# Sliding-window attention on quarter tiles of TensorE, in a fused attention and snake-MLP kernel on one core

## The chip, the cores and the metric

The kernel runs on one core of one Trainium2 chip. TensorE multiplies matrices (its weight loads are counted apart, as PEld), ACT evaluates functions such as exp and sine, DVE does elementwise work and reductions, GpSimd (POOL) and SyncE issue transfers. The metric is the device time of one execution in microseconds. Times per stage come from one profiled execution.

## The reference: what is computed

There are 8 batches, 8 heads, 576 positions and 64 elements per head. Scores are kept within 32 positions of the diagonal and in the rows and columns of 8 global positions; all else is masked away. The attention output becomes 4608 tokens of 512 features, and an MLP with a snake activation follows.

```python
scores = scale * np.matmul(q, k.transpose(0, 1, 3, 2))
mask = np.abs(pos[:, None] - pos[None, :]) <= window
mask = mask | is_global[:, None] | is_global[None, :]
attn = softmax(np.where(mask, scores, -1e9))
x = (attn @ v).transpose(0, 2, 1, 3).reshape(B * S, H * D)
h = x @ w_in                      # 512 -> 2048
s = np.sin(alpha * h)
out = (h + s * s / (alpha + 1e-9)) @ w_out   # 2048 -> 512
```

## The kernel before, in words

**Tiles of attention.** Keys of a head are cut into 12 tiles of 48. A key tile meets a window of 120 query columns (`WCOL`): twice 60, for the even and the odd positions, with 4 columns for global queries in each 60. Each key tile also carries the 8 global keys, so 56 of 64 rows are in use. Two heads form a pair (`NHP` = 4 pairs). A pair is worked on as one 128 x 128 matmul with two zero blocks: `KX` holds the keys of head 0 in rows and columns 0 to 63 and of head 1 in rows and columns 64 to 127, zeros elsewhere, and `VX` likewise for the values. Per pair, `scores` (line 739) runs 12 such matmuls of 120 columns in three groups of 4, each into a PSUM bank of a ring of two. ACT takes exp of a group (line 747), with a sum over the row as a second result, which an instruction of its own reads out. DVE multiplies by the 0/1 mask (line 750). `products` (line 781) multiplies the result E with the values (key 0, into the tile `zn`) and with `OB`, two blocks of ones (key 1, into `zd`, the denominators); 2 of the 12 windows cross the middle and are cut in two, so there are 14 matmuls per key. `inverse` (lines 807 and 810) makes 1/denominator as exp(-ln), `normalise` (line 813) multiplies, and `sums` (line 791) adds up the partial rows of the global queries.

**The MLP.** `gemm1` (line 969) multiplies 4 x 128 weights blocks of `w_in` with the 576 tokens of a batch for each of 16 blocks of hidden features, in halves of 288 columns; the blocks take the PSUM tiles `zn`, `zr`, `zd` in turn. ACT takes the sine, ACT or DVE squares it, DVE adds h (line 1016). `gemm2` (line 1029) is a generator: each step is one matmul of 512 columns, and every 16 steps ACT copies a result (line 1035) that SyncE stores.

**The order.** Nothing reorders the program; each engine runs its instructions in the order in which they are written. `phase_a(b+1, b)` emits the attention of batch b+1, and pours in steps of `gemm2(b)` with `fill(n)`: `START` steps before the first scores, `PER_SCORES` after each group, `MIDST` near the end, 53 in all for most batches; `gemm1` takes 16 more (`PER_GROUP`). For the attention of batch 1 there are other numbers (`LATE`, `GROUP_LATE`). What isn't used up is carried on, and the last of it follows the last batch. `products` of a pair come one pair later than its scores. `warm` issues matmuls without use where the attention has nothing beside it.

**Loads.** GpSimd issues, in one queue: V straight into `VX` (`load_v`, line 390, 4 transfers a pair, 16 a batch), the casts of K and Q to bf16 in DRAM (`cast_qk`, line 328), the weights (lines 407 and 413), and copies of global keys and queries (`place_globals`, lines 368 and 373). SyncE issues the transposes of the casts (`turn_qk`, line 337), the global rows of V (`load_vg`, line 399, 8 a batch), gathers, and the stores. Each queue has 8 semaphores for its transfers, and a transfer waits for the one that used its semaphore before, eight earlier. In the attention of batch 0, a copy of one element (`seen`) holds GpSimd until the transpose for batch 1 has landed; after it come the second half of `w_in` and V of batch 1. Batch 0's K and Q go through TensorE transposes (line 587).

**Guards.** The kernel keeps bounds for the whole run and takes a general path if one is broken: row sums of exp (`EA`) and of the inverses (`RA`), and the norm of each token against the largest column norm of `w_in` times alpha (`square_x`, `token_norms`, `square_w`, `column_norms`, `judge`), since the sine takes limited arguments. The general path didn't run in any execution shown.

Of the kernel before, what the change touches and what calls it, by code (L numbers as in the profile page):

```python
# [16 lines left out]
P = 128  # L17
# [12 lines left out]
LIM_SUM = float(2.0**50)  # L30
LIM_REC = float(2.0**40)
TINY = float(2.0**-60)
# [215 lines left out]
def kernel(  # L248
# [16 lines left out]
    NT12 = S // KT  # L265
    NHP = H // 2
# [19 lines left out]
    pairp = mctx.enter_context(tc.tile_pool(name="pairp", bufs=2))  # L286
# [4 lines left out]
    srp = mctx.enter_context(tc.tile_pool(name="srp", bufs=4))  # L291

    VX = [main.tile([P, NHP, NT12, P], DT.bfloat16, name=f"VX{i}") for i in range(2)]
    KX = [main.tile([P, NHP, NT12, P], DT.bfloat16, name=f"KX{i}") for i in range(2)]
# [6 lines left out]
    OB = main.tile([P, P], DT.bfloat16, name="OB")  # L301
    MASK = main.tile([P, NT12, WCOL], DT.bfloat16, name="MASK")
# [7 lines left out]
    tiny = main.tile([P, 1], DT.float32, name="tiny")  # L310
    SQ = main.tile([P, CT * S], DT.bfloat16, name="SQ")
    W2 = main.tile([P, DFF], DT.bfloat16, name="W2")
    limit = main.tile([P, 1], DT.float32, name="limit")
    EA = main.tile([P, B * NHP * 3], DT.float32, name="EA")
    RA = main.tile([P, B * NHP], DT.float32, name="RA")
    XC = main.tile([P, B], DT.float32, name="XC")
    XCG = main.tile([P, 1], DT.float32, name="XCG")
# [24 lines left out]
    def place(b, which, t, y, copy, hps=slice(0, NHP)):  # L342
# [10 lines left out]
        else:  # L353
            copy(
                out=KX[b % 2][rows, hps, :, t * D + y * 24 : t * D + y * 24 + 24],
# [8 lines left out]
    def place_globals(b):  # L364

        for t in range(2):
            rows = slice(t * D, (t + 1) * D)
            nc.gpsimd.tensor_copy(
                out=KX[b % 2][rows, :, :, t * D + KT : t * D + KT + NG],
                in_=kTg[rows, :, None, :, b].to_broadcast([D, NHP, NT12, NG]),  # L370
            )
        for y in range(2):
            nc.gpsimd.tensor_copy(
                out=globals_of(b, slice(0, P), y),
                in_=qTg[:, :, None, y::2, b].to_broadcast([P, NHP, 7, 4]),
            )
# [8 lines left out]
    def load_v(b, hps=range(NHP)):  # L385
        for hp in hps:
            for t in range(2):
                for y in range(2):
                    r = t * D + y * 24
                    nc.gpsimd.dma_start(  # L390
                        out=VX[b % 2][r : r + 24, hp, :, t * D : t * D + D],
                        in_=v[b, 2 * hp + t].rearrange("(i a y) d -> y a i d", a=24, y=2)[y],
                    )

    def load_vg(b):
        for h in range(H):
            t = h % 2
            src = VGb[b::B, h * D : (h + 1) * D] if b else VG0[h::H]
            nc.sync.dma_start(
                out=VX[b % 2][t * D + KT : t * D + KT + NG, h // 2, :, t * D : t * D + D],  # L400
                in_=src[:, None, :].to_broadcast([NG, NT12, D]),
            )
# [48 lines left out]
    qpos = setup.tile([P, NT12, 2, 24], DT.float32, name="qpos")  # L451
    nc.gpsimd.iota(qpos[:], pattern=[[KT, NT12], [1, 2], [2, 24]], base=0, channel_multiplier=0,
# [40 lines left out]
    def clear(t):  # L493
        n = t.shape[1]
        nc.scalar.activation(out=t, in_=zero[:].to_broadcast([P, n]), func=AF.Copy, scale=0.0)

    nc.scalar.preload_act_table_set("natural_log_exp_and_others")
    clear(QX[0][:].rearrange("p h y c -> p (h y c)").bitcast(DT.float32))
    vflat = VX[0][:].rearrange("p h i c -> p (h i c)").bitcast(DT.float32)
    kflat = KX[0][:].rearrange("p h i c -> p (h i c)").bitcast(DT.float32)  # L500
# [689 lines left out]
```

## Time and profile before

| | |
|---|---|
| median of 3 runs | 381.93 us (381.09 to 382.87) |
| profiled execution, span from first to last instruction | 379.3 us, 8582 instructions |
| median less that span | 2.6 us |
| mean granted TensorE clock | 0.994 |
| transfers | 38.08 MB in 103579 packets |

The time of the profiled execution is known as its span; what lies around it is taken from the median. In rows of groups, the columns are line, engine, operation, output and inputs, shapes and count, then busy time in us and mean ns of one, then idle time before them and what ended it. In the timeline they are start, length, engine, line, group, and idle time before it in brackets. A matmul's length has its way through the array in it, so that a group's length is more than its count times the pace.

### The profile page before, as it was taken

The page shows a single profiled execution, that of the slowest core. Times are in us where ns is not written, and L with a number is a line of the kernel's source. Part 1 is how long each engine was busy: PE and PEld are TensorE (multiplying, and loading weights), DVE is VectorE, ACT ScalarE, POOL GpSimd, SP SyncE. Part 2 cuts the span into 40 slices and gives each one's busy share as a digit, 9 for nine tenths or more (in the row PEclk, how much of TensorE's full clock was granted, in tenths as well). Part 3 has the DMA queues.
Part 4 walks back from the last instruction along what each step waited for, and adds up shares of the span by engine and source line. Part 5 has one row for each costly group of instructions (what it writes and reads, how often), then busy time and mean ns, then how long its engine had stood idle before and what let it go on. Part 6 is the DMA issues. An engine that isn't in the chain of part 4 may idle for free. (4 is left out here: it accounts for less than half of the span.)

```text
span 379.3 us, 8582 instructions
## 1 busy us (share of the span) xinstructions
PE 338.6 (89%) x3124; PEld 231.9 (61%) x3172; DVE 288.8 (76%) x615; ACT 294.0 (77%) x563; POOL 130.4 (34%) x203
## 2 busy tenths in 40 slices
PE   2578967998998899899989999999999998999893
PEld 2466645765566666676666766676676665775341
DVE  5787897589789887988888788888888876589400
ACT  6889797899889688788878887879788888675110
POOL 7981695677277002840086007720000000000001
PEclk9999999999999999999999999999999999999997
DMA  7998999999988772799069923828111010101221
GB/s 121 117 184 172 152 166 173 170 207 146 204 163 76 134 124 65 92 109 204 28 85 105 193 58 45 84 31 156 50 35 29 0 55 32 29 3 29 56 84 48
DMA packets 103579, 38.08 MB, mean 100 GB/s; under 512 B 94138, under 2 KB 98250, under 8 KB 103082
## 3 DMA queue, kind: packets, MB, share of 16 engines
q0 software_dynamic: 56640, 18.56, 42.2%
q1 hardware_dynamic: 46890, 18.89, 23.1%
q8 instruction: 27, 0.44, 0.5%
q14 instruction: 22, 0.18, 0.2%
HBM read 37.15 MB, written 17.83 MB: 145 GB/s over the span
## 5 line engine op out<-in xcount | busy, mean ns | idle before, releaser
L1029 PE MATMUL zo<-w_out,H 128*128 128x512 bf16 x528 | 142.5, 378 | 2.0
L969 PEld LDWEIGHTS <-w_in 128*128 128x128 bf16 x1024 | 99.2, 97 | 49.3 <-issue 17.6
L390 POOL DMA_DIRECT2D VX<-in_v_dram x128 | 84.0, 667 | 106.5 <-PE zd L781 89.6
L1029 PEld LDWEIGHTS <-H 128*128 128x128 bf16 x576 | 52.0, 97 | 37.3
L747 ACT ACTIVATE E<-ring 128x480 bf16<-128x480 f32 x96 | 54.2, 568 | 23.3 <-PE ring L739 22.8
L969 PE MATMUL zn<-xT,w_in 128*128 128x288 bf16 x384 | 57.3, 285 | 5.6 <-DVE H L1016 4.1
L969 PE MATMUL zr<-xT,w_in 128*128 128x288 bf16 x320 | 47.9, 285 | 1.3 <-DVE H L1016 0.6
L969 PE MATMUL zd<-xT,w_in 128*128 128x288 bf16 x320 | 46.6, 285 | 1.7 <-DVE H L1016 1.7
L750 DVE TENSOR_TENSOR E<-E,MASK 128x480 bf16<-128x480 bf16 x96 | 36.0, 408 | 14.8 <-ACT E L747 13.5
L1016 DVE SCALAR_TENSOR_TENSOR H<-s,recipT,zn 128x576 bf16<-128x576 bf16 x48 | 39.1, 814 | 10.5 <-ACT s L1010 6.2
L1005 ACT ACTIVATE sb<-zn,alphaT 128x576 bf16<-128x576 f32 (+1 forms) x48 | 35.6, 742 | 13.3 <-PE zn L969 9.8
L1057 POOL DMA_INDIRECT out_dram<-osb,grow x1 | 1.0, 1007 | 126.1 <-SPq L1158 126.1
L1010 ACT ACTIVATE s<-sb 128x576 bf16<-128x576 bf16 (+1 forms) x62 | 42.7, 689 | 2.0
L739 PE MATMUL ring<-QX,KX 128*128 128x120 bf16 x384 | 37.2, 221 | 7.1 <-ACT E L747 4.2
L739 PEld LDWEIGHTS <-KX 128*128 128x128 bf16 x384 | 28.2, 100 | 22.0 <-issue 9.0
L1016 DVE SCALAR_TENSOR_TENSOR H<-s,recipT,zd 128x576 bf16<-128x576 bf16 x40 | 32.5, 813 | 6.5 <-ACT s L1010 4.8
L1016 DVE SCALAR_TENSOR_TENSOR H<-s,recipT,zr 128x576 bf16<-128x576 bf16 x40 | 32.5, 813 | 5.0 <-ACT s L1010 2.8
L1012 DVE TENSOR_TENSOR s<-sb 128x576 bf16<-128x576 bf16 (+1 forms) x66 | 30.8, 467 | 7.0 <-ACT sb L1005 6.7
L1035 ACT COPY osb<-zo 128x512 f32<-128x512 f32 x36 | 20.8, 578 | 19.5 <-PE zo L1029 19.4
L1005 ACT ACTIVATE sb<-zd,alphaT 128x576 bf16<-128x576 f32 (+1 forms) x40 | 29.7, 742 | 7.5 <-PE zd L969 4.7
L1005 ACT ACTIVATE sb<-zr,alphaT 128x576 bf16<-128x576 f32 (+1 forms) x40 | 29.6, 740 | 5.1 <-PE zr L969 3.8
L781 PEld LDWEIGHTS <-VX 128*128 128x128 bf16 x448 | 25.9, 98 | 12.2 <-issue 6.7
(157 smaller groups left out, 446.8 us busy)
## 6 DMA issues: line engine op xcount, KB each, us to landing
VX<-in_v_dram POOLq DMA_DIRECT2D x128, 36.0 KB, 3.6
kd<-in_k_dram POOLq DMA_DIRECT2D x7, 576.0 KB, 6.2
qd<-in_q_dram POOLq DMA_DIRECT2D x7, 576.0 KB, 8.9
w_in<-in_moe_w_in_dram POOLq DMA_DIRECT2D x4, 512.0 KB, 5.7
w_out<-in_moe_w_out_dram POOLq DMA_DIRECT2D x4, 512.0 KB, 8.7
out_dram<-osb SPq DMA_DIRECT2D x8, 256.0 KB
out_dram<-osb SPq DMA_DIRECT2D x8, 224.0 KB
out_dram<-osb SPq DMA_DIRECT2D x8, 192.0 KB
```

The costliest lines, as they stand in the source:

```text
L390: nc.gpsimd.dma_start(out=VX[b % 2][r : r + 24, hp, :, t * D : t * D + D], in_=v[b, 2 * hp + t].rearrange("(i a y) d -> y a i d", a=24, y= ...
L739: nc.tensor.matmul(out=ps[:, e * WCOL : (e + 1) * WCOL], lhsT=kx[:, hp, i, :], rhs=qx[:, hp, :, s0 : s0 + 60], start=True, stop=True, skip ...
L747: nc.scalar.activation(out=Eg, in_=ps[:, 0 : 4 * WCOL], func=AF.Exp, scale=scale, accum_out=EA[:, n : n + 1])
L750: nc.vector.tensor_tensor(out=Eg, in0=Eg, in1=MASK[:, 4 * g : 4 * g + 4, :].rearrange("p i c -> p (i c)"), op=ALU.mult,)
L781: nc.tensor.matmul(out=out_t[:, half, :, a - half * CUT : z - half * CUT], lhsT=OB[:] if key else VXb[:, hp, i, :], rhs=E[:, i, :, a - s0 ...
L969: nc.tensor.matmul(out=h[:, e, 0:HALF], lhsT=lhsT, rhs=xT[:, c, e, :], start=(c == 0), stop=(c == CT - 1), skip_group_check=True,)
L1005: nc.scalar.activation(out=sb[:, :, 0:W], in_=h[:, :, 0:W], func=AF.Sin, scale=alphaT[:, nt : nt + 1])
L1010: nc.scalar.activation(out=s2[:, :, 0:W], in_=sb[:, :, 0:W], func=AF.Square)
L1012: nc.vector.tensor_tensor(out=s2[:, :, 0:W], in0=sb[:, :, 0:W], in1=sb[:, :, 0:W], op=ALU.mult)
L1016: nc.vector.scalar_tensor_tensor(out=dst.rearrange("p (e c) -> p e c", e=2), in0=s2[:, :, lo:hi], scalar=recipT[:, nt : nt + 1], in1=h[:, ...
L1029: nc.tensor.matmul(out=ops[:], lhsT=H2[:, nt, blk * P : (blk + 1) * P], rhs=w_out[:, nt, :], start=(nt == 0), stop=(nt == NT - 1),)
L1035: nc.scalar.copy(out=osb[:], in_=ops[:])
```

## The change

**Attention tiles.** The zero blocks go. Each 64-row half of the partitions and each 64-column half of the array is used by a matmul of its own: rows by head in `scores`, columns by which half of the sequence. Key tile m and key tile m+6 stand one below the other in the output, so that scores of a pair take two banks (one per head) of 3 x 120 columns, in two groups. Windows that cross the middle of the sequence are computed for both halves. In `products`, rows are the halves of the sequence and columns the heads. Both use 28 matmuls of 64 x 64 (or 56 x 64) weights per pair and key where there were 12 or 14 of 128 x 128.

**Exponentials** are taken over two banks at once, 720 elements a row, twice a pair, without row sums; the ring of two score tiles becomes one tile of two banks. **Products and inverse** come later: denominators one pair behind the scores, values two pairs behind (near the end closer). **Logarithms** of the denominators are copied to `LC` by SyncE, and the guard tests these. **Token norms** come from a matmul of each 64 tokens with themselves (Gram matrix), whose largest entry DVE keeps; the squares on DVE go; the squares of `w_in` move to the end, before a longer `judge`. The reciprocals for the global rows are taken for 7 batches at once and for the last.

**Loads.** V is loaded per head, half and parity: 32 transfers a batch of 24 x 7 x 64 in place of 16 of 24 x 12 x 64; the tile m = 5 to 6 around the middle comes twice. The global rows of V come in 2 transfers a batch in place of 8, in batch 0 in 16. Clears of `VX`, `QX` and `KX` go or shrink, and `place_globals` writes the keys in one copy.

**Fills** are 47 a batch in place of 53.

```diff
-        def scores(hp, g):
-                nc.tensor.matmul(
-                    out=ps[:, e * WCOL : (e + 1) * WCOL],
-                    lhsT=kx[:, hp, i, :],
-                    rhs=qx[:, hp, :, s0 : s0 + 60],
...
+        zs = ring.tile([P, 2, 512], DT.float32, name="ring")
+        def windows(half):
+            last = half * (NT6 - 1)
+            return [(half * NT6 + m, m, 16 * (m == 0 == half), 60 - 16 * (m == half * last > 0)) for m in range(NT6)] + [
+                (NT6 - half, last, 44 * half, 16 + 44 * half)
+            ]
+        def scores(hp, g):
+            for e in range(NT6 + 1):
+                for half in range(2):
+                    i, m, c0, c1 = windows(half)[e]
+                    if m // G3 != g:
+                        continue
+                    for t in range(2):
+                        rows = slice(t * D, (t + 1) * D)
+                        nc.tensor.matmul(
+                            out=zs[half * D : (half + 1) * D, t, 0 : G3 * WCOL].rearrange(
+                                "p (m x c) -> p m x c", x=2, c=60
+                            )[:, m % G3, :, c0:c1],
+                            lhsT=kx[rows, hp, i, :],
+                            rhs=qx[rows, hp, :, s0 + c0 : s0 + c1],
...
+            nc.scalar.activation(out=Eg, in_=zs[:, :, 0 : G3 * WCOL], func=AF.Exp, scale=scale)
...
+        def products(hp, key):
+            for e in range(NT6 + 1):
+                for half in range(2):
+                    rows = slice(half * D, half * D + NK)
+                    for t in range(2):
+                        nc.tensor.matmul(
+                            out=nd(hp, key)[t * D : (t + 1) * D, half, :, a - half * CUT : z - half * CUT],
+                            lhsT=ones[rows, 0:D] if key else VXb[rows, i - half * (NT6 - 1), 2 * hp + t, :],
...
+        def logarithm(hp):
+            nc.scalar.activation(out=Ls[hp][:], in_=body(hp, 1), func=AF.Ln)
+            nc.sync.dma_start(
+                out=LC[r0 : r0 + 2, :], in_=Ls[hp][0:P:D].rearrange("p k m c -> p (k m c)")
+            )
+            sums(hp, 1)
...
+            scores(hp, 0)
+            if hp > 1:
+                inverse(hp - 2)
+                products(hp - 2, 0)
+                normalise(hp - 2)
+            fill(first[hp])
+            scores(hp, 1)
+            if hp:
+                products(hp - 1, 1)
+                logarithm(hp - 1)
+            fill(second[hp])
...
+    def token_norms(b, z):
+        xf = xTs[b][:].rearrange("p c e s -> p c (e s)")
+        for j in range(5):
+            for c in range(CT):
+                for side in range(2):
+                    cols = slice(min(2 * j + side, 8) * D, min(2 * j + side, 8) * D + D)
+                    nc.tensor.matmul(
+                        out=z[side * D : (side + 1) * D, 0, j * D : (j + 1) * D], lhsT=xf[:, c, cols],
+                        rhs=xf[:, c, cols], start=(c == 0), stop=(c == CT - 1), skip_group_check=True,
+                    )
+        nc.vector.tensor_reduce(out=XC[:, b : b + 1], in_=z[:, 0, 0 : 5 * D], axis=AX.X, op=ALU.max)
...
     def load_v(b, hps=range(NHP)):
+            for h in (2 * hp, 2 * hp + 1):
+                for half in range(2):
+                    for y in range(2):
+                        nc.gpsimd.dma_start(
+                            out=VX[b % 2][r : r + 24, :, h, :],
...
-    START = 2
-    PER_SCORES = ((1, 11, 3), (3, 3, 4), (3, 3, 4), (3, 4, 5))
-    LATE = ((0, 0, 0), (0, 0, 0), (2, 3, 3), (4, 4, 6))
-    MIDST = 4
+    START = 4
+    FIRST, SECOND = (5, 5, 5, 5), (4, 4, 4, 3)
+    LATE_FIRST, LATE_SECOND = (0, 0, 3, 5), (0, 0, 3, 4)
+    NEAR, MIDST = 2, 6
...
+    token_norms(B - 1, zn)
+    global_norms(zd)
+    judge_sums()
     fill(16)
-    judge(zn[:, 0, :])
+    xm = largest_norm(zd)
+    for c in range(CT):
+        square_w(c)
+        fill(16)
+    judge(zn, xm)
```

More of the change, by code (lines that the diff above doesn't have):

```diff
@@ L309 @@
     grow = main.tile([NG * B, 1], DT.int32, name="grow")
[L310 to L317, printed above, removed]
+    LC = main.tile([B * H, S], DT.float32, name="LC")
+    GD, GN, GR = [main.tile([P, NHP, NG, B], DT.float32, name=name) for name in ("GD", "GN", "GR")]
+    XC = main.tile([P, B + 1], DT.float32, name="XC")
     cast = {}
@@ L364, in place_globals @@
     def place_globals(b):
[L366 to L371, printed above, removed]
+        nc.gpsimd.tensor_copy(
+            out=KX[b % 2][:, :, :, KT:NK], in_=kTg[:, :, None, :, b].to_broadcast([P, NHP, NT12, NG])
+        )
         for y in range(2):
@@ L821, in idle @@
                 warm(zo[0], 1)
+        start, first, second = (START, FIRST, SECOND) if b != 1 else (0, LATE_FIRST, LATE_SECOND)
         fill(start)
@@ L943, in judge @@
-        nc.vector.tensor_copy(out=verdict[:], in_=pv[:, 0:1])
+        nc.vector.tensor_reduce(out=okb[:], in_=oks[:], axis=AX.X, op=ALU.min)
+        nc.tensor.matmul(out=z[:, 1, 0:1], lhsT=ones[:], rhs=okb[:], start=True, stop=True)
+        nc.vector.tensor_copy(out=verdict[:], in_=z[:, 1, 0:1])
     ON_ACT = (1, 3, 5, 8, 10, 12, 14)
@@ L1065, in fill @@
     def fill(n):
-        while n and waiting:
+        done = 0
+        while done < n and waiting:
             if next(waiting[0], None) is None:
```

328 lines of the change are left out of this document (133 added, 195 removed).

## The prediction

> **What bounds the kernel now.** I read the page first (busy shares, slices), then the windows of single stages, then the timeline of TensorE inside one stage, last the queues of GpSimd and SyncE in the first 60 us. "Stage n" is the attention of batch n (0 to 7), with the second GEMM of batch n-1 poured between its matmuls; "GEMM n" is the first GEMM of batch n.
>
> ```profile
> PE 338.6 (89%) x3124; PEld 231.9 (61%) x3172; DVE 288.8 (76%) x615; ACT 294.0 (77%) x563; POOL 130.4 (34%) x203
> DMA  7998999999988772799069923828111010101221
> ...
> 99.10:119.70 20.60, 19.07 (x209) 12.50 (x211) 16.03 (x34) 18.34 (x41) 10.98 (x16) 1.00 0.96 158
> ...
> 182.20:202.10 19.90, 18.86 (x211) 12.62 (x213) 16.72 (x37) 16.23 (x41) 10.86 (x16) 1.00 0.51 63
> 262.70:281.50 18.80, 18.63 (x209) 12.56 (x212) 15.38 (x37) 15.72 (x41) 0.00 (x0) 1.00 0.25 57
> 301.90:320.70 18.80, 18.63 (x210) 12.57 (x213) 13.05 (x31) 16.21 (x41) 0.00 (x0) 1.00 0.13 44
> ```
>
> The windows are stages 2, 4, 6 and 7: length, then PE, weight loads, DVE, ACT, POOL busy, granted clock, DMA share. In stages 6 and 7 TensorE is busy 18.63 of 18.80 us at full clock; ACT has 2.6 us left, DVE 3.4 and more. Stages 2 and 4 are 1.8 and 1.1 us longer, with TensorE waiting. So a stage is as long as its TensorE stream. The DMA line is over 0.8 for most of the first half: at the start, loads are the other limit.
>
> **TensorE's part.** Pace is start of a group to start of the next.
>
> ```profile
> 277.75 0.37 PE L739 MATMUL ring<-QX,KX 128*128 128x120 bf16 x4
> 277.96 0.36 PE L781 MATMUL zn<-E,VX 128*128 128x120 bf16 x4
> ...
> 279.43 0.79 PE L781 MATMUL zr<-E,OB 128*128 128x88 bf16 x14
> 280.06 1.03 PE L1029 MATMUL zo<-w_out,H 128*128 128x512 bf16 x4
> 280.92 0.79 PE L781 MATMUL zd<-E,VX 128*128 128x88 bf16 x14
> ```
>
> Scores: 0.21/4 = 52 ns each. Products: 0.63/14 = 45 ns. A fill (512 columns): 0.86/4 = 0.215 us. So a stage spends 48 x 52 + 112 x 45 = 2.5 + 5.0 = 7.5 us on attention. The change makes these 112 + 224 = 336 matmuls on quarter tiles (7 positions x 2 halves x 2 heads; once for scores, twice for products; 4 pairs of heads), each with its weight load. No row shows quarter tiles in parallel. Bounds come from these:
>
> ```profile
> 145.67 0.54 PE L880 MATMUL zn<-ones,W 128*128 128x1 bf16 x16
> 146.08 0.37 PE L739 MATMUL ring<-QX,KX 128*128 128x120 bf16 x4
> ...
> 354.68 0.28 PE L921 MATMUL zd<-sg,ones 128*128 128x64 bf16 x4 [0.82 <-DVE sg L919]
> 354.79 3.62 PE L1029 MATMUL zo<-w_out,H 128*128 128x512 bf16 x15
> ...
> 365.83 3.40 PE L1029 MATMUL zo<-w_out,H 128*128 128x512 bf16 x14
> 369.16 3.64 PE L1051 MATMUL zo<-w_out,HG 128*64 128x512 bf16 x16
> ...
> 369.16 3.16 PEld L1051 LDWEIGHTS <-HG 128*64 128x64 bf16 x16 [0.42 <-issue]
> ...
> L723 ACT ACT_TABLE_LOAD x7 | 9.0, 1283 | 0.1
> ```
>
> A pair of weight load and one-column matmul takes 0.41/16 = 25.6 ns, of 64 columns 27.5. Four tiles truly at once cost 45 ns for four: 11 ns each, 3.8 us a stage. Pairs that go one by one cost 25.6: 8.6 us. If nothing overlaps, 45: 15.1 us. I take 15 ns, **5.0 us**, nearer to 11 than to 25.6, because the four tiles share neither rows and columns nor, across row halves, a PSUM bank.
>
> The change also changes the tile shape: fills use the whole array, attention a quarter. L1051 is the one switch in the trace between long matmuls. From 365.83 to 369.16 are 3.33 us, 15 fills of 0.2155 (one record is missing) and 0.10 us more, and the weight load that otherwise runs ahead sat idle 0.42 us and began only with its matmul. A stage has 11 blocks of tiled matmuls between fills, and the block of norms changes shape once more: 23 switches x 0.10 = **2.3 us** (between 0, if the queue hides them, and 23 x 0.15).
>
> The Trainium skill, "TensorEngine Tiling (Array Packing)", sections Tiling Modes and Tile-to-Partition Mapping, says that changing the mode drains TensorE and that column tiling turns Fast Weight Load off; both speak against this change, and L1051's late weight load agrees with the first.
>
> Token norms: 40 matmuls of 64 columns at 27.5 ns are 1.1 us, 0.55 if two column tiles overlap: 0.8, less the 288-column matmul that goes (288/512 of a fill, 0.1): **+0.7**. The fills between the first two score groups fall from 11 to 5, and these 11 cover the load of ACT's exp table (1283 ns a load), which exp and hence the second scores wait for, as there is now one score tile: 6 x 0.215 = 1.3 us of cover lost, of which the fills put ahead give back some: **+0.5**. The other six of a stage's 53 fills that move go to the end, where TensorE runs them at the same pace: 0 in the sum.
>
> One stage: -7.5 + 5.0 + 2.3 + 0.7 + 0.5 = +1.0. Stages 2 to 7: **+6.0**.
>
> **ACT and DVE.**
>
> ```profile
> L747 ACT ACTIVATE E<-ring 128x480 bf16<-128x480 f32 x96 | 54.2, 568 | 23.3 <-PE ring L739 22.8
> L747 ACT ACTIVATION_READ_ACCUMULATOR E<-ring 128x1 f32 x96 | 19.0, 198 | 0.0
> L810 ACT ACTIVATION_READ_ACCUMULATOR R<-L 128x1 f32 x32 | 6.0, 187 | 0.0
> L902 DVE TENSOR_TENSOR SQ<-SQ 128x1152 bf16<-128x1152 bf16 (+1 forms) x16 | 11.8, 741 | 0.3
> L899 DVE TENSOR_TENSOR SQ<-xT 128x2304 bf16<-128x2304 bf16 x8 | 10.8, 1351 | 0.0
> ```
>
> ACT loses 12 x (568 + 198) + 4 x 187 = 9.9 us a stage and gets 8 exponentials of 720 elements, some 0.85 each (568 x 720/480): -3.1. DVE loses 1.35 + 2 x 0.74 and more. That is off the path where TensorE is 99% busy; it pays where a stage waits. Stages 2 to 5 are like the two quoted, 1.1 to 1.8 us longer than stage 6. I take **-3.2** for these four (0 to -5.5). The added single score tile makes scores wait for exp; behind it in TensorE's queue stand the products and fills. Products, fills and switches between two score groups last 1.5 us, exp and its neighbour on ACT about as much, so the wait is near zero but without reserve. The new stores of logarithms wait on SyncE for Ln, with output stores behind them; three output buffers cover that: 0.
>
> **The start.** V is loaded in 32 transfers a batch, not 16.
>
> ```profile
> 19.57 2.71 POOL L390 DMA_DIRECT2D VX<-in_v_dram  x4
> 22.28 0.55 POOL L328 DMA_DIRECT2D kd<-in_k_dram  x1
> ...
> 36.18 0.49 POOL L1096 COPY seen<-kt 1x1 bf16<-1x1 bf16 x1 [8.96 <-DMA kt<-kd]
> 36.63 1.54 POOL L407 DMA_DIRECT2D w_in<-in_moe_w_in_dram  x2
> ...
> 42.57 0.65 POOL L390 DMA_DIRECT2D VX<-in_v_dram  x1 [0.51 <-DMA w_in<-in_moe_w_in_dram]
> ...
> 52.36 0.91 POOL L373 COPY QX<-qTg 128x112 bf16<-128x112 bf16 x2
> ...
> 15.88 5.43 SPq L399 DMA_DIRECT2D VX<-VG  x8
> ...
> 31.52 2.27 SPq L337 DMA_TRANSPOSE kt<-kd  x1
> ...
> 43.42 1.14 PE L969 MATMUL zd<-xT,w_in 128*128 128x288 bf16 x8
> ...
> 55.70 0.37 PE L739 MATMUL ring<-QX,KX 128*128 128x120 bf16 x4 [0.63 <-DVE H L1016]
> ...
> kd<-in_k_dram POOLq DMA_DIRECT2D x7, 576.0 KB, 6.2
> ```
>
> All of this is one queue in order. 16 more issues at 0.55 (kd) to 0.68 (2.71/4), say 0.6, move kd's issue from 22.28 to 31.9; it lands 6.2 later, at 38.1. SyncE is there too late as well: 8 more global rows of V cost 5.4 us ahead of the transpose. So kt's transpose begins 6 us later than 31.52, "seen" and the second half of w_in follow, and w_in's third group lands at 48.6, not 42.57. GEMM 0 needs it at 43.42 (the third zd group, its ninth of sixteen): 5 us lost. Behind that, GpSimd issues 8 more V transfers (4.8 us) before it writes the global keys and queries that stage 1 reads: 53.3 + 6 + 4.8 = 64, against the 55.70 at which stage 1 begins now. Of these 8 us, stage 1 and GEMM 1 win back about 2.5 (less ACT work; the squares of w_in leave GEMM 1). The removed clears, memsets and block padding lie in time in which the first matmuls wait for K: 0. **+5.5** (2 to 9). Later, 9.6 us more of issues in a 40 us period fit: POOL is busy 10.86 of stage 4's 19.9.
>
> The end has two waits of TensorE on DVE in its norm chain, like the 0.82 at L921, where one goes: **+1**.
>
> **Sum.** 6.0 - 3.2 + 5.5 + 1.0 = +9.3 on a span of 379.3: 388.6. The median of the runs shown, 381.93, is 2.6 over that span: **391** us.
>
> **Rivals.** (a) *The tiles don't overlap*, so the change does not do what it says: pairs at 25.6 ns, +10.6 x 336 = 3.6 us a stage, x 6 = 21: 412; at 45 ns 451. For it: the floor stands in two rows, whatever the width. Against: both are of one tile. (b) *Faster*: tiles at 11 ns (-1.3 a stage) and switches at half price (-1.15), so -15 in six stages: 376, about where ACT's and TensorE's chain of scores and exp binds. It decides from the point where 336 matmuls and 23 switches take under 5.75 us a stage together (7.3 in the forecast). For it: ACT and DVE have room for it; against: L1051's row. (c) *Tiles at 11 ns, switches at full price*: 391 - 8 = 383.
>
> The Trainium skill, "TensorE: Matmul & The Clock Gate", Part 3, gives starts of tiles some 4 ns apart and a span of one matmul plus that; no run here shows it; by it (c) holds.
>
> **How the numbers follow.** Forecast 0.42 (385 to 398). (a) 0.24 at 412 and 0.04 far beyond; (b) 0.22; (c) 0.08. The range runs from (b)'s 376 to just above (a)'s 412, 416, and leaves out half of (b) and the far end of (a). A measurement can tell about 0.5% from no change: slower 0.42 + 0.28 = 0.70, same 0.08, faster 0.22.
>
> **What would show it.** Groups of 28 products in the timeline: 0.42 us right, 0.3 for (b) and (c), 0.7 for (a). The gap between a fill and the tiled group behind it: 0.10 over its pace. Stage 6 at 18.5 us (19.8 less 6 fills). w_in's third group in use at 48 us and stage 1's first scores past 60; if they stay at 43 and 56, that term is wrong. Exp waiting for scores, not scores for exp, with ACT under 85% in a stage. Wrong in all: a stage under 17 us.

## The result, and the profile after

The changed kernel takes **416.26 us** (median of 4 runs, 414.27 to 419.65) against 382.13 us for the kernel before in runs beside it (4 runs): a ratio of 1.0889, 95% interval [1.0807, 1.0971]. The profiled execution took 417.47 us with a span of 415.8 us (before: 379.3). The direction was predicted; the size, +9.3 us, was not: it is +34, just outside the range.

First the page of the changed kernel: the busy line, the clock, the DMA share and the costliest group.

```profile
PE 333.9 (80%) x4829; PEld 215.8 (52%) x4890; DVE 261.8 (63%) x526; ACT 273.6 (66%) x400; POOL 195.8 (47%) x322
...
PEclk9997559969999999999999999999999999989997
DMA  8879989589999799777936895686111010001221
...
L382 POOL DMA_DIRECT2D VX<-in_v_dram x256 | 161.5, 637 | 63.7 <-PE zn L777 34.0
```

TensorE, VectorE and ScalarE all have *less* work than before, and GpSimd 65 us more: 161.5 of its 195.8 us are the issuing of V's transfers, 637 ns each (84.0 before). The clock line holds two 5s in the fifth and sixth slice (42 to 62 us): there TensorE stood still long enough to lose its clock. So the loss is a wait near the start. The timeline says the same, by when each stage begins:

| us from the span's start | before | after | difference |
|---|---|---|---|
| stage 0 | 16.1 | 15.6 | -0.5 |
| GEMM 0 | 33.3 | 60.2 | +26.9 |
| stage 1 | 55.7 | 83.6 | +27.9 |
| stage 2 | 99.2 | 129.8 | +30.6 |
| end of GEMM 7 | 345.5 | 367.7 | +22.2 |
| end of the span | 379.3 | 415.8 | +36.5 |

Thirty microseconds are lost before stage 2, eight come back between there and the end of GEMM 7, and fourteen go at the end. The eight are mostly not a gain: 36 fills (six in each of stages 2 to 7, 36 x 0.2155 = 7.8 us) moved to the end. These are the windows of stages 6 and 7 (length; PE, weight loads, DVE, ACT, POOL busy; clock; DMA):

```profile
287.00:304.70 17.70, 16.11 (x415) 9.41 (x421) 12.40 (x28) 14.15 (x22) 0.00 (x0) 1.00 0.15 42
325.60:343.20 17.60, 16.01 (x416) 9.34 (x421) 11.12 (x23) 14.21 (x22) 0.00 (x0) 1.00 0.17 48
```

Stage 6 lasts 17.7 us. Between its first scores and the GEMM behind it stand 43 fills where there were 51 (of the 47 and 53 a batch, four and two now come before the first scores); with these eight (1.7 us) it would be 19.5, against 18.8 before, and 18.6 without the wait of 0.82 us shown below, which experiment e8 comes back to. So the new attention costs about what the old one did. TensorE is busy 16.11 of 17.70 where it was busy 18.63 of 18.80: some 1.6 us of each stage are no longer work.

**The start**, in the timeline of the changed kernel (start, duration, engine, line, operation, out<-in, count, and in brackets the idle time before it and what ended it; SPq is SyncE's DMA queue):

```profile
15.95 11.30 SPq L398 DMA_DIRECT2D VX<-VG  x16
...
40.64 3.48 SPq L331 DMA_TRANSPOSE kt<-kd  x1
...
46.41 6.77 SPq L483 DMA_DIRECT2D H<-in_v_dram  x8
53.28 6.97 SPq L805 DMA_DIRECT2D LC<-L  x4
...
35.25 0.57 POOL L322 DMA_DIRECT2D kd<-in_k_dram  x1
...
46.16 0.18 POOL L1104 COPY seen<-kt 1x1 bf16<-1x1 bf16 x1 [9.83 <-DMA kt<-kd]
...
76.27 0.87 POOL L360 COPY KX<-kTg 128x384 bf16<-128x384 bf16 x1 [11.30 <-DVE kTg L695]
...
57.84 0.65 ACT L803 ACTIVATE L<-zd 128x576 f32<-128x576 f32 x1 [27.01 <-DMA LC<-L]
...
58.81 1.19 PE L777 MATMUL zd<-E,VX 56*64 56x88 bf16 x28 [26.39 <-DMA VX<-in_v_dram]
...
129.81 0.35 PE L739 MATMUL ring<-QX,KX 64*64 64x88 bf16 x14 [1.43 <-POOL QX L364]
```

Read it from the wait backwards. ScalarE's third Ln stands still for 27.01 us, because the tile for logarithms has two buffers, and the first is free only when SyncE has copied it into LC. The four copies stand in SyncE's queue behind everything issued before them: 16 global rows of V, the gather of q, two transposes that wait for kd, and the gather of v. So the first starts at 53.28, some 29 us after its logarithm was ready. TensorE waits for that Ln, and for a short sum of DVE behind it, to free zd. Its row names V's transfer as the releaser, but batch 0's last one was issued at 34.63, and none of V's took more than 9.8 us to land: the name is an inference, and Ln's own row beside it decides. In the kernel before, the third Ln waits for nothing:

```profile
30.90 0.73 ACT L807 ACTIVATE L<-zd,tiny 128x576 f32<-128x576 f32 x1
```

The prediction's first doubt is there as well. kd is issued at 35.25 (forecast 31.9), the transposes start at 40.64 (31.52 before), "seen" follows at 46.16 (36.18). But in this profile it hides behind the other wait, so which of the two is paid can't be read here. That is what the first experiments are for.

The cost of the stop goes on at half clock. The windows of the three stretches in which the granted clock fell, and, second, of the 3.7 us ahead of the second one:

```profile
36.10:63.40 27.30, 4.41 (x43) 2.99 (x43) 2.14 (x6) 3.84 (x5) 14.12 (x23) 0.50 1.00 145
83.60:87.30 3.70, 1.96 (x68) 1.48 (x70) 2.39 (x5) 3.10 (x4) 3.70 (x7) 0.98 0.63 40
87.30:94.20 6.90, 6.20 (x152) 4.03 (x151) 5.93 (x16) 3.51 (x6) 6.15 (x10) 0.52 0.88 140
370.60:374.10 3.50, 3.15 (x49) 2.17 (x51) 2.12 (x6) 0.00 (x0) 0.00 (x0) 0.53 0.00 0
```

After a wait TensorE is busy and yet slow: 6.20 of 6.90 us at a clock of 0.52. The Trainium skill, "TensorE: Matmul & The Clock Gate", Part 1, says that an idle window of about 3.4 us halves the clock and that it comes back after as long a busy one. The first stretch agrees: TensorE's last matmul before it ends at 32.4 and the clock falls near 36; work begins again at 58.81 and the clock comes back near 63.3. The other two don't fit so simply. The third begins inside a wait of 2.96 us. Ahead of the second, TensorE was busy 1.96 of 3.70 us, with no wait above 1.71 us (stage 1's scores for an exponential, at 86.01). Being half idle is not enough by itself, though: in e9, TensorE is busy only 1.05 of the 3.70 us from 118.5 to 122.2, with a wait of 2.65 us, and the clock stays at 1.00. What decides in these cases is not shown.

**Inside a stage**, from the timeline of TensorE in stage 6:

```profile
289.28 0.35 PE L739 MATMUL ring<-QX,KX 64*64 64x120 bf16 x14 [0.82 <-ACT E L748]
289.56 1.04 PE L1037 MATMUL zo<-w_out,H 128*128 128x512 bf16 x4
...
292.94 0.49 PE L777 MATMUL zd<-E,ones 56*64 56x88 bf16 x28
293.36 0.82 PE L1037 MATMUL zo<-w_out,H 128*128 128x512 bf16 x3
...
294.52 0.65 PE L777 MATMUL zn<-E,VX 56*64 56x88 bf16 x28
295.10 1.25 PE L1037 MATMUL zo<-w_out,H 128*128 128x512 bf16 x5
```

The group of 28 products that was to last 0.42 if the forecast held (0.3 for the faster rivals, 0.7 for the slower) lasts 0.42 with the ones (292.94 to 293.36) and 0.58 with the values, both with the change of tile shape behind them, which the forecast had counted apart. The second score group waits 0.82 us for the first exponential, which stands behind the table load: the cover that the prediction saw going.

### The profile page after: what moved, and what is told of

Its sections match the earlier page's. It is cut to its first block, busy times and chain, and to the rows that moved or that the text cites. A ratio compares the mean times of both kernels' runs of the same rounds, so it can differ in the third digit from the quotient of the medians.

```text
span 415.8 us, 12016 instructions
## 1 busy us (share of the span) xinstructions
PE 333.9 (80%) x4829; PEld 215.8 (52%) x4890; DVE 261.8 (63%) x526; ACT 273.6 (66%) x400; POOL 195.8 (47%) x322
## 5 line engine op out<-in xcount | busy, mean ns | idle before, releaser
L382 POOL DMA_DIRECT2D VX<-in_v_dram x256 | 161.5, 637 | 63.7 <-PE zn L777 34.0
L1037 PE MATMUL zo<-w_out,H 128*128 128x512 bf16 x515 | 138.2, 382 | 4.8 <-issue 3.9
L981 PEld LDWEIGHTS <-w_in 128*128 128x128 bf16 x1024 | 99.7, 98 | 47.1 <-issue 14.3
L1037 PEld LDWEIGHTS <-H 128*128 128x128 bf16 x576 | 50.9, 98 | 45.8 <-issue 2.9
L748 ACT ACTIVATE E<-ring 128x720 bf16<-128x720 f32 x64 | 49.4, 772 | 31.5 <-PE ring L739 30.9
L981 PE MATMUL zn<-xT,w_in 128*128 128x288 bf16 x384 | 58.2, 288 | 4.2 <-DVE H L1024 3.5
L749 DVE TENSOR_TENSOR E<-E,MASK 128x720 bf16<-128x720 bf16 x64 | 34.7, 543 | 29.8 <-ACT E L748 29.3
L1020 DVE TENSOR_TENSOR s<-sb 128x576 bf16<-128x576 bf16 (+1 forms) x66 | 33.4, 506 | 10.1 <-ACT sb L1013 10.0
L777 PEld LDWEIGHTS <-VX 56*64 56x64 bf16 x896 | 18.7, 113 | 38.4 <-DMA VX<-in_v_dram 28.8
L739 PE MATMUL ring<-QX,KX 64*64 64x120 bf16 (+2 forms) x896 | 24.8, 225 | 16.4 <-ACT E L748 11.6
L739 PEld LDWEIGHTS <-KX 64*64 64x64 bf16 x896 | 18.2, 114 | 37.5 <-issue 35.6
```

The costliest lines, as they stand in the source:

```text
L382: nc.gpsimd.dma_start(out=VX[b % 2][r : r + 24, :, h, :], in_=v[b, h].rearrange("(m a y) d -> y a m d", a=24, y=2)[y, :, half * (NT6 - 1) ...
L739: nc.tensor.matmul(out=zs[half * D : (half + 1) * D, t, 0 : G3 * WCOL].rearrange("p (m x c) -> p m x c", x=2, c=60)[:, m % G3, :, c0:c1], ...
L748: nc.scalar.activation(out=Eg, in_=zs[:, :, 0 : G3 * WCOL], func=AF.Exp, scale=scale)
L749: nc.vector.tensor_tensor(out=Eg, in0=Eg, in1=MASK[:, None, G3 * g : G3 * (g + 1), :].rearrange("p o m c -> p o (m c)").to_broadcast([P, 2 ...
L777: nc.tensor.matmul(out=nd(hp, key)[t * D : (t + 1) * D, half, :, a - half * CUT : z - half * CUT], lhsT=ones[rows, 0:D] if key else VXb[ro ...
L981: nc.tensor.matmul(out=h[:, e, 0:HALF], lhsT=lhsT, rhs=xT[:, c, e, :], start=(c == 0), stop=(c == CT - 1), skip_group_check=True,)
```

## The experiments

**e1: four buffers for the logarithms** in the changed kernel.

```
+    logp = mctx.enter_context(tc.tile_pool(name="logp", bufs=4))
...
-            Ls[hp] = normp.tile([P, 4, 3, KT], DT.float32, name="L")
+            Ls[hp] = logp.tile([P, 4, 3, KT], DT.float32, name="L")
```

> The changed kernel, with four buffers for the logarithm tile L in place of two (a pool of its own); nothing else. Theory 1: in stage 0 the third Ln waits 27 us because both L buffers are held by copies to LC that stand in SyncE's queue behind the transposes and gathers for batch 1. With four buffers that wait goes; the next limits are then V of the last pair, whose last transfer is issued at 35 us, and the third group of w_in, which lands near 52. GEMM 0 ends near 63 instead of 83, and GpSimd's global keys let stage 1 begin near 66.5 instead of 83.6: 17 us less, 399 (394 to 403). Theory 2, the releaser that the trace names for TensorE's 26.4 us wait (a V transfer): V is late and the L buffers do not matter: 416, within 2.

Measured: 412.81 us (408.17 to 413.96), ratio 1.0786 [1.0699, 1.0873]. Only 3.5 us came back of a wait of 27. GEMM 0 begins at 36.0 instead of 60.2, stage 1 at 66.8 instead of 83.6, but stage 2 at 122.5 instead of 129.8. The timeline shows what took the place of the wait:

```profile
121.71 0.69 POOL L365 COPY QX<-qTg 128x112 bf16<-128x112 bf16 x2
...
122.45 0.51 PE L740 MATMUL ring<-QX,KX 64*64 64x88 bf16 x14 [11.13 <-POOL QX L365]
```

Stage 2 waits 11.13 us for the global queries that GpSimd writes, in its own order, behind batch 2's 32 transfers of V, two casts and eight transfers for batch 3. So neither theory as written held: the wait for the buffer is real, and something as large stands right behind it.

**e2: the same copies issued by ScalarE**, which has just written the logarithms, with two buffers.

```
-            nc.sync.dma_start(
+            nc.scalar.dma_start(
                 out=LC[r0 : r0 + 2, :], ...
```

> The changed kernel, with the copies of the logarithms issued on ACT's queue in place of SyncE's; L keeps two buffers. Theory 1 (SyncE's queue order holds the copies): the same gain as with four buffers, some 399, plus 32 issues on ACT that lie in its idle time (0 to 3 us). If it is the copies as such, or their time to land, that make ACT wait, and not the queue they stand in: 416.

Measured: 413.3 us (2 runs), ratio 1.0821 [1.076, 1.0882]; GEMM 0 at 36.2 and stage 2 at 122.5, as in e1; the figure of 399 fell with e1's. That confirms from another side that it was SyncE's queue, not the copying, that held the buffers, and that this alone is worth little here.

**e3 and e4: the kernel before, with one suspect each.** e3 adds the copies of the logarithms to SyncE's queue (with the tile LC that they go to) and nothing else of the change; e4 loads V in 32 transfers a batch and changes nothing else.

```
e3:
+            nc.sync.dma_start(
+                out=LC[r0 : r0 + 2, :], in_=L[0:P:D].rearrange("p k m c -> p (k m c)")
+            )
e4:
+                    for i in (0, 6):
                         nc.gpsimd.dma_start(
-                            out=VX[b % 2][r : r + 24, hp, :, t * D : t * D + D],
+                            out=VX[b % 2][r : r + 24, hp, i : i + 6, t * D : t * D + D],
```

> The kernel before, with one part of the change alone: the copies of two rows of each logarithm tile to LC through SyncE, L with its two buffers. The copies change no result. Theory 1: the third Ln of stage 0 (30.9 us) has to wait for the first copy, which SyncE issues only after its gathers of V, at 43.3, and which lands some 2 us later: GEMM 0 starts 14 to 15 us later, 396 (393 to 399). Theory 2 (late V transfers): 382, within 1.5.

> The kernel before, with V loaded in 32 transfers a batch (24 x 6 x 64) in place of 16 of 24 x 12 x 64; the same bytes, no tile twice. By the prediction's term for the start: 16 more issues ahead of the casts, w_in's third group lands 6 to 8 us after its use at 43.4 in GEMM 0, of which 5.5 (2 to 9) stay: 388 (384 to 391). Rival: the issues are hidden in GpSimd's wait for the transposed keys (8.96 us): 382, within 1.5.

Measured: e3 400.95 us (400.36 to 407.08), ratio 1.0486 [1.0435, 1.0536]; e4 408.89 us (406.41 to 416.89), ratio 1.0706 [1.0651, 1.076]; the kernel before beside them 381.88. So **the copies cost 19 us and the split of V 27 us**, each by itself, and each more than any theory had put down. e3's timeline repeats the picture of the changed kernel:

```profile
44.12 8.32 SPq L810 DMA_DIRECT2D LC<-L  x4
...
49.77 0.74 ACT L808 ACTIVATE L<-zd,tiny 128x576 f32<-128x576 f32 x1 [19.84 <-DMA LC<-L]
```

and e4's shows where most of the 27 us are lost:

```profile
32.61 0.55 POOL L328 DMA_DIRECT2D kd<-in_k_dram  x1
...
44.92 0.18 POOL L1097 COPY seen<-kt 1x1 bf16<-1x1 bf16 x1 [7.38 <-DMA kt<-kd]
...
65.88 0.69 POOL L373 COPY QX<-qTg 128x112 bf16<-128x112 bf16 x2
...
118.23 0.69 POOL L373 COPY QX<-qTg 128x112 bf16<-128x112 bf16 x2
...
66.62 0.37 PE L740 MATMUL ring<-QX,KX 128*128 128x120 bf16 x4 [1.81 <-POOL QX L373]
...
118.98 0.56 PE L740 MATMUL ring<-QX,KX 128*128 128x120 bf16 x4 [8.22 <-POOL QX L373]
```

kd, the global operands of stage 1 and those of stage 2 all stand behind V in one queue. Stage 1 begins at 66.6, 10.9 us late, and stage 2 at 119.0, 19.8 us late: **the queue is paid twice**, and the prediction had dated only the first time. The other 5.5 us of its span come later and were not taken apart.

**e5: V in 16 transfers again**, on e1. With the keys of a tile in natural order in KX and V, one transfer a head and half brings 48 keys of 7 tiles.

```
-                out=KX[b % 2][rows, hps, :, y * 24 : y * 24 + 24],
+                out=KX[b % 2][rows, hps, :, y:KT:2],
...
-                    for y in range(2):
-                        r = half * D + y * 24
-                        nc.gpsimd.dma_start(out=VX[b % 2][r : r + 24, :, h, :], ...
+                    r = half * D
+                    nc.gpsimd.dma_start(out=VX[b % 2][r : r + KT, :, h, :], ...
...
```

The positions of the keys in the window mask follow the new order.

> Four buffers for L, and V in 16 transfers a batch (48 x 7 x 64): the 48 keys of a tile stand in their natural order, so that one transfer takes even and odd keys; keys and the window mask follow that order, the result does not change. Bytes and packets as in the changed kernel. Theory 1 (the number of transfers ahead of others in GpSimd's queue sets the start): w_in and the global keys come as early as before, stage 2 starts near 101 instead of 122.5, 391 (387 to 396). Theory 2 (bytes and packets, the DMA engines are full): 412, within 3.

**e6: the order of GpSimd's queue alone**, on e1: batch 1's casts right behind the first eight transfers of V, and stage 2's global operands written together with stage 1's.

```
     load_w_in((0,))
+    cast_qk(1)
     load_v(0, (1, 2))
...
-    cast_qk(1)
...
                 place_globals(1)
+                place_globals(2)
...
-            place_globals(b + 1)
+            if b > 1:
+                place_globals(b + 1)
```

> Four buffers for L, V still in 32 transfers, but two things moved ahead in GpSimd's queue: the casts for batch 1 stand behind the first 8 V transfers instead of behind all 32, and the global keys of batch 2 are written with those of batch 1, ahead of V of batch 2. Theory 1: GEMM 0 has its weights in time and stage 1 starts near 60 instead of 66.8; the wait of stage 2's first scores for the global queries (11 us) goes, stage 2 starts near 106 instead of 122.5: 397 (391 to 402). Theory 2 (full DMA engines): 412, within 3.

Measured: e5 401.24 us (396.4 to 404.7), ratio 1.0479 [1.0344, 1.0614], stage 2 at 112.2; e6 401.78 us (400.23 to 404.58), ratio 1.0556 [1.0482, 1.0629], stage 2 at 111.5. By the medians, half the issues are worth 11.6 us against e1 and the same issues in another order 11.0 (the intervals are 3 to 5 us wide on each side, so that the two can't be told apart): what counts is not GpSimd's load but what stands behind it. Both miss their figure (391 and 397), as the next queue takes over. e5's rows of SyncE:

```profile
16.03 10.62 SPq L398 DMA_DIRECT2D VX<-VG  x16
27.27 10.31 SPq L483 DMA_DIRECT2D H<-in_q_dram  x8
37.69 2.21 SPq L332 DMA_TRANSPOSE kt<-kd  x1
```

The transposes start at 37.69 though kd was issued at 22.6: SyncE is busy with 16 global rows of V, eight more than before, and the gather. In e6 it is the same: the 16 rows hold SyncE from 16.2 to 32.7, and the transposes start at 40.2.

**e7 and e8: the end and the stages.** e7 puts 16 fills ahead of the last batch's norms (on e5); e8 gives four fills more a stage to the wait for the first exponential (on e7).

```
e7:
     waiting.append(gemm2(B - 1))
+    fill(16)
     token_norms(B - 1, zn)

e8:
-    FIRST, SECOND = (5, 5, 5, 5), (4, 4, 4, 3)
+    FIRST, SECOND = (9, 5, 5, 5), (4, 4, 4, 3)
```

> As with V in 16 transfers, and 16 fills ahead of the last batch's token norms, which now wait 2.96 us for DVE's last H with nothing in between; the clock falls to half for 3.4 us behind that wait. Theory: the wait and the half clock go, 4 us less than with V in 16 (3 to 5). Rival: the fills only change places with the wait (DVE's chain of checks becomes the bound): within 1.

> As the run with 16 fills ahead of the norms, and 9 fills in place of 5 behind the first score group of a stage (stages 2 to 7), where the second score group waits some 0.8 us for exp, which waits for its table. Theory (the term of +0.5 a stage was right): 0.5 to 0.8 us a stage, 3 to 5 us less than without. Rival: the four fills, taken from the end of the queue, cost the stage as much as they hide: within 1.

Measured: e7 398.64 us (394.65 to 402.76), ratio 1.0415 [1.031, 1.0519]; e8 392.22 us (391.6 to 393.15), ratio 1.0299 [1.0267, 1.0332]. e7's 2.6 us lie within the spread of its runs, though its end is 3.3 us shorter in the profile (45.2, from 48.5). What it takes away is this wait at the end of the changed kernel, which was followed by the stretch at half clock:

```profile
370.62 1.28 PE L888 MATMUL zn<-xT 128*64 128x64 bf16 x40 [2.96 <-DVE HG L1024]
```

e8's 6.4 us, more than the 3 to 5 expected, are clear, as each of its runs lies below each of e7's: 24 fills (5.2 us) leave the end (39.9, from 45.2), and stage 6 still lasts 17.6 us. They cost the stages next to nothing (0.7 us from stage 2 to the end of GEMM 7), as they run in the 0.82 us that the scores waited.

**e9: batch 0's global rows of V through DRAM**, on e8: one write, then one read for each half, 3 transfers of SyncE for 16.

```
-            for h in range(H):
-                nc.sync.dma_start(
-                    out=VX[0][r : r + NG, :, h, :], in_=VG0[h::H, None, :].to_broadcast([NG, NT6 + 1, D])
-                )
+            if r == KT:
+                vgd = dramp.tile([NG, H * D], DT.bfloat16, name="vgd")
+                nc.sync.dma_start(out=vgd[:].rearrange("j (h d) -> (j h) d", d=D), in_=VG0[:])
+            nc.sync.dma_start(
+                out=VX[0][r : r + NG].rearrange("p m h d -> p m (h d)"),
+                in_=vgd[:][:, None, :].to_broadcast([NG, NT6 + 1, H * D]),
+            )
```

> The kernel of e8, with batch 0's global rows of V brought in by three transfers of SyncE (the gathered rows written to DRAM once, then read back once for each half with all tiles) where 16 stood. In e8 those 16 hold SyncE from 16.2 to 26.9, the gather of global queries ends at 37.8, the transposes of batch 1's keys start at 37.9 (31.5 in the kernel before), GpSimd waits for them until 43.9, and stage 2 starts at 110.1 (99.2 before). Theory that SyncE's queue is what is left of the late start: the rows are there by 22, the transposes start at 31 to 33, GpSimd goes on at about 38, stage 2 starts at 102 to 104, 384 to 386 us. Rival, that something else (the placing of the operands, the exponentials, the idle clock) sets the pace of the start: stage 2 at 109 to 110, 391 to 392 us.

**e10: the kernel before with both suspects** of e3 and e4.

> The kernel before with both of the changes that cost most in e3 and e4: the copies of the logarithms in SyncE's queue (401.0 alone, +19) and V in 32 transfers of GpSimd (408.9 alone, +27). If the two delays hide one another, because both hold back the same stages of the start: 407 to 414 us. If they add: 428 us.

**e11: e9 with two buffers for the logarithms again**, as in the changed kernel.

> The kernel of e9 with two buffers for the logarithms again, as in the changed kernel. With the queue shorter, what stands ahead of the copies on SyncE (the gather of queries, two transposes, the gather of values) is still there until about 43, while stage 0 wants its third buffer at about 33: theory that the wait for the buffer is a cost of its own, once V's loads no longer hide it: 5 to 10 us above e9. Rival, that e9's start has a cover for it: within 1 us of e9.

Measured, on one chip with the kernel before at 382.43 us: e9 **386.14 us** (384.56 to 388.68), ratio 1.0125 [1.007, 1.0179]; e10 416.22 us (411.53 to 421.04), ratio 1.0849 [1.0773, 1.0925]; e11 402.9 us (400.96 to 403.49), ratio 1.0531 [1.0489, 1.0573].

e9 came out at its figure (384 to 386): the timeline has the transposes at 30.27 and "seen" 8 us earlier than in e8 (43.9), and stage 2 begins at 105.0 where 102 to 104 was expected.

```profile
20.77 0.64 SPq L400 DMA_DIRECT2D VX<-vgd  x2
21.62 7.29 SPq L486 DMA_DIRECT2D H<-in_q_dram  x8
30.27 3.07 SPq L332 DMA_TRANSPOSE kt<-kd  x1
...
35.67 0.18 POOL L1106 COPY seen<-kt 1x1 bf16<-1x1 bf16 x1 [11.84 <-DMA kt<-kd]
```

e10 says two things. The delays **hide one another in part**: 19 and 27 us alone, 34 together, 2 more than was expected if they hide and 12 less than if they add. And the kernel before with these two edits alone is as slow as the whole changed kernel (416.22 and 416.26 us, each ratio known to some 3 us): the two side effects of the change on the queues are enough to make a loss of this size. It doesn't follow that the rest of the change is worth nothing, as delays that hide one another can hide the rest too: the 16 global rows on SyncE, for one, are worth 6.1 us in e9 once the others are gone.

e11 is the counterpart to e1. The second pair of buffers, worth 3.5 us while V's transfers stood behind, is worth 16.8 us once they don't, more than the 5 to 10 expected; the rival, that the start covers it, fell. Its Ln in the timeline:

```profile
45.16 7.76 SPq L807 DMA_DIRECT2D LC<-L  x4
...
50.51 0.65 ACT L805 ACTIVATE L<-zd 128x576 f32<-128x576 f32 x1 [17.45 <-DMA LC<-L]
```

**e12: the idle time of the start filled**, on e9: 33 fills in stage 1 for 15, no warming matmuls there, and the second half of batch 0's operands copied in two parts.

```
-    LATE_FIRST, LATE_SECOND = (0, 0, 3, 5), (0, 0, 3, 4)
+    LATE_FIRST, LATE_SECOND = (8, 3, 4, 5), (3, 3, 3, 4)
...
+                if at in (0, 1):
+                    second_half(at)
                 if at == 0:
-                    second_half()
```

> The kernel of e9 with the idle time of the start given to work. Stage 1 takes 33 fills of the second GEMM where it took 15, and none of its five warming matmuls of 0.55 us (2.7 us in all, beside 2.7 us of waits, 1.78 of them for the exponentials behind the table load), and the second half of batch 0's operands is copied in two parts, one after each of the first two head pairs, where one block of eight copies (3.9 us on ScalarE) held back the exponentials and PE waited 4.0 us. Theory that TensorE is now the bound from stage 1 to the end, so that only its idle time is left to win: 18 fills x 0.2155 = 3.9 us that stage 1 takes nearly for nothing, and 0 to 2 us in stage 0: 381 to 383 us, as the kernel before or just under it. Rival, that stage 1 is paced by the exponentials and the placing, so that the fills only move: 385 to 387 us.

Measured: 388.71 us (387.64 to 390.36), ratio 1.0189 [1.0158, 1.022], the kernel before at 382.04. The theory's figure (381 to 383) fell, and the rival's (385 to 387) as well: stage 1 grew by 2.7 us (22.4, from 19.7), GEMM 1 shrank by 0.8 only, and stage 2 began 3 us later. The timeline of stage 1 shows what neither had foreseen:

```profile
73.17 0.24 PE L740 MATMUL ring<-QX,KX 64*64 64x120 bf16 x1
75.70 0.34 PE L740 MATMUL ring<-QX,KX 64*64 64x120 bf16 x11 [2.30 <-issue]
...
82.45 0.26 PE L778 MATMUL zd<-E,VX 56*64 56x120 bf16 x9 [1.94 <-issue]
```

Twice TensorE stops in the middle of a group of matmuls, and the profile shows nothing that it waits for ("issue"). The two stops are 4.2 us, more than stage 1 grew by, and e9 has one such stop in stage 0 (1.82 us) but none in stage 1. What they are, and whether the fills would have paid without them, is not shown, so e12 decides neither for the theory nor for the rival. No version here beats the kernel before.

## Why the prediction was wrong

By its own steps, with what the runs gave.

**"The new stores of logarithms wait on SyncE for Ln ... three output buffers cover that: 0."** This step failed outright. It looked at who waits behind the new copies (the output stores), not at what the copies wait behind, nor at the tile that they hold: two buffers of logarithms, freed by a queue that in the first 50 us is full of loads. 19 us alone in e3, 27.01 us of wait in the changed kernel, 16.8 us in e11 against e9.

**"The start: +5.5 (2 to 9)."** Half right. The dates of the queue came out within 4 us in e1: kd, forecast for 31.9, is issued at 32.95; the third group of w_in, forecast in use at 48, at 51.8; stage 1's global operands, forecast for 64, are written from 64.4 on, and stage 1 begins at 66.8, 11.1 us late. What failed is what followed from them. "Stage 1 and GEMM 1 win back about 2.5": they won nothing and lost 12 more, stage 2 begins 23.3 us late in e1. And **"Later, 9.6 us more of issues in a 40 us period fit"**: the argument took GpSimd's share of busy time, where its order decides. Until stage 2 the queue is late already, each transfer waits for an earlier one to land, and the copies that stage 2 needs stand behind them. 27 us alone in e4; in e6 the same issues in a better order, 11 us less.

**The tiles, 5.0 us a stage, and the switches, 2.3.** Right in mechanism, somewhat high in size. In stage 6 of e9, where nothing waits, the timeline has:

```profile
270.02 1.04 PE L1039 MATMUL zo<-w_out,H 128*128 128x512 bf16 x4
270.99 0.35 PE L741 MATMUL ring<-QX,KX 64*64 64x88 bf16 x14
271.18 0.48 PE L779 MATMUL zn<-E,VX 56*64 56x88 bf16 x28
271.58 1.25 PE L1039 MATMUL zo<-w_out,H 128*128 128x512 bf16 x5
272.77 0.35 PE L741 MATMUL ring<-QX,KX 64*64 64x120 bf16 x14
```

14 scores take 0.19 us, 28 products with the switch behind them 0.40, and four fills 0.97 where they alone take 0.86: 0.11 for the switch into the tiles. So scores go at some 14 ns each and products, less 0.1 for the switch, at 11. In the changed kernel the products with the values took 0.58 ahead of fills, and 0.58 or more in the other runs that split V in this way (e1, e2, e6), against 0.40 to 0.43 in the runs with V in 16 transfers (e5, e7 to e9, e11). The rows of their weight loads in stage 6 hold 16 semaphore instructions of 51 ns in the changed kernel, e1 and e6, and 2 in e5 and e9; four of them a group are about the 0.18 us that differ. So this is no pace of the tiles but, by these rows, a small cost of V's many transfers on TensorE. Eight groups of scores (0.19), eight of products with a switch behind (0.40), eleven switches into tiles (0.11) and three out of scores into fills (0.1: ahead of a fill 14 scores last 0.28 to 0.29) come to 1.5 + 3.2 + 1.2 + 0.3 = 6.2 us a stage: between the forecast's 7.3 and the 5.75 from which rival (b) was to decide. Rival (a), that the tiles don't overlap, is out: 25.6 ns a pair would have been 0.7 us a group. The Trainium skill's rule from "TensorEngine Tiling (Array Packing)", Tiling Modes, that a change of mode drains TensorE, is in line with the 0.11. That of "TensorE: Matmul & The Clock Gate", Part 3, by which the four of a set nearly share one matmul's time, agrees: 4 x 11 to 14 ns is 43 to 54 ns, and a full-width product took 45, a full-width score 52. So rival (c), 11 ns with switches at full price, had the products right; its 383 us fell with the queues.

**Norms +0.7 and exponential cover +0.5.** The 40 norm matmuls take 0.75 us in the changed kernel (290.53 to 291.28), the wait is 0.82. Both right, but the second is no cost of the change: e8 filled it for next to nothing.

**Stages 2 to 7: +6.0, and -3.2 of waits in stages 2 to 5.** Their sum, +2.8, was to be the change from the start of stage 2 to the end of GEMM 7. Measured is 237.9 us against 246.3, and with the 7.8 us of fills that moved, -0.6. Stage 6, forecast at 18.5 with six fills fewer, lasts 17.7 with eight fewer: +0.6 where +1.0 was forecast. Together, stages 2 to 5 were 5.3 us longer than four stages 6 before and are 2.1 longer after, the forecast's -3.2 (though in e9 it is 5.1 again). With the 0.82 filled and the queues mended (e9) it is 238.5 with 12 fills fewer (2.6 us), so -5.2. The windows of e9's stages 6 and 7 show why there is little more to win there:

```profile
263.60:281.20 17.60, 17.20 (x425) 9.35 (x425) 13.59 (x28) 14.06 (x22) 0.00 (x0) 1.00 0.19 49
301.80:319.00 17.20, 17.20 (x425) 9.27 (x425) 11.17 (x23) 14.30 (x22) 0.00 (x0) 1.00 0.16 49
```

TensorE is busy 17.20 of 17.60 and 17.20 of 17.20 us; the work that ScalarE lost lies beside it.

**The end: +1.** Mis-sized. The end is 14.3 us longer; 39 fills more (137 against 98 by the kernels' own counts; the rows, of which some are missing, show 133 and 95) are 8.4 of it, as the prediction put them at no cost in the sum. Of the other 6, 2.96 are the wait at the first norms and 1.6 the half clock behind it (3.5 us at 0.53); the last 1.3 were not taken apart.

**The sum.** Predicted +2.8 + 5.5 + 1.0 = +9.3. Measured, moved fills set off: 30.6 for the start, -0.6 for the stages, 6 for the end: 36 on the span. The stage, on which most of the working went, was within 4 us in six stages; the queues, to which it gave a paragraph and one clause, hold 30. The verdict "slower" was right for a reason that was mostly not its own: in that it was lucky.

e9's remaining 3.6 us on the span are made up so: stage 2 begins 5.9 us late, the stretch from there to the end of GEMM 7 is 7.8 shorter (2.6 of it 12 fills fewer), and the end is 5.6 longer (3.2 of it 15 fills more, these 12 and three of stage 1). Whether the start can be had back with the new layout of K and V stays open.

## What to carry to other kernels

A transfer added to an in-order queue is priced by what stands behind it and by which buffer it holds until it runs, at the fullest time of that queue; the share of time that the engine is busy says nothing of it. Follow each new transfer to the first instruction that waits for its buffer or for its successors, batch by batch until the queue is idle again, not only to the first one. Two delays of the same stages can hide one another: undoing one alone can show little (3.5 us here), so put each one alone into the kernel *before*, and take the last one out once the others are gone.

## What the runs showed of the hardware

- Four quarter tiles with a weight load each run at 11 to 14 ns a matmul (43 to 54 ns a set of four) in stage 6 of e9, and a change from whole-array fills to tiles costs about 0.11 us there, a change back about 0.10.
- In the changed kernel a transfer cost GpSimd 0.53 to 0.79 us of issuing with little regard to its size (0.64 for V's 21 KB, 0.55 for kd's 576 KB, 0.79 for w_in's 512 KB); V's landed 2.8 us later in the median. Batch 1's first transpose began 5.4 us after the cast that it reads was issued, and 9.2 us after it in the kernel before, with SyncE free earlier in both.
- The granted clock halved not only in the wait of 27 us but in two stretches more (6.9 and 3.5 us at 0.52 and 0.53), in which TensorE was busy nine tenths of the time; the longest waits ahead of these were 1.71 and 2.96 us. In e9 a wait of 2.65 us didn't halve it.
- A releaser named by the trace can be wrong by a whole chain: TensorE's 26.39 us were put down to a transfer that had landed, and ended with ScalarE's Ln and DVE's sum behind it.
